# Reordering a gated-attention and expert kernel: decay issues, first loads, state scaling, transposes, and the last expert's second layer

## The chip, the cores and the metric

The kernel runs on one core of a Trainium2 chip. The metric is the device time of one execution in microseconds, from launch to end; lower is better. The core has TensorE (PE, with its weight loads shown apart as PEld), VectorE (DVE), ScalarE (ACT), GpSimd (POOL) and SyncE (SP, which here only issues DMAs). ACT and POOL issue DMAs too. Each engine takes its own instructions in order; semaphores hold an instruction until what it needs is there.

## The reference

Two blocks, one after the other, in float32. First a gated recurrence over 4 batches, 8 heads, 768 steps, head dimension 48:

```python
for t in range(S):
    state = alpha[:, :, t, :, None] * state + np.einsum('bhd,bhe->bhde', k[:, :, t], v[:, :, t])
    y[:, :, t] = np.einsum('bhd,bhde->bhe', q[:, :, t], state)
```

Its output, as 3072 rows of 384, goes through a layer of 8 experts with one expert for each row:

```python
expert_idx = np.argmax(x @ w_gate, axis=1)
gate_w = probs[np.arange(N), expert_idx]
# for each expert e, with its rows of x:
h = np.maximum(x_sorted[lo:hi] @ w1[e], 0.0)     # 384 -> 1024
y_sorted[lo:hi] = h @ w2[e]                      # 1024 -> 384
# back in the rows' own order, times gate_w
```

## The kernel before, in words

**The token loop.** The 768 steps of 4 batches are 24 tiles of 128 steps of one batch (8 heads side by side, 384 columns); tile s is chunk s // 4 of batch s % 4. The recurrence is done by chunks. For a tile, ACT takes the logarithm of alpha (`logs`, L387), PE sums it along the steps (`cums`, L393), ACT makes the running product `cp` and its inverse `icp` (L396, L397), and POOL multiplies q and k with them (`operands`, L434; the first tile on DVE). PE turns both (`transposes`, L444; ACT or DVE copies them out as kT and qT, L448 and L450), forms the scores (`scores`, L457), DVE masks them (L465), and PE adds to the PSUM tile `y` what comes from the earlier chunk's state (`read_state`, L484), from within the tile (`attend`, L494), and the keys times values for the new state (`keys_values`, L505). `result` (L513, ACT) copies y out as yT; `rows` (L531, PE) turns it into token rows `x` and gate logits in one PSUM bank; `gate`, `gate_weight` make the row's weight, and `keep_rows` (L556, ACT) copies x times that weight to `xs`, which SP stores to DRAM (L557).

The state's decay from one chunk to the next needs one row of `icp` and one of `cp` of every tile. `cums` sends them to a small tile `dec` with two DMAs issued by ACT (L405); POOL multiplies the rows (`decay_rows`, L413 and L414), PE turns them (L425), DVE copies the columns (`E`, L427), and `scale_state` (L472, POOL) scales the old state to U, which `read_state` uses.

The order is written out by hand. The loop runs over i from -4 to 23 with these stages of neighbouring tiles in each turn, and no scheduler moves them: in turn i, scores of tile i, transposes of i + 1, operands of i + 2, rows of i - 1, keep_rows of i - 2, running sums up to tile i + 5. Loads are issued by SP (`loads_for`), single tiles for the first two of each of alpha, k, q, v, then pairs of tiles (384 KB). `idle` (L589) is a filler: matmuls on zeros at the start. Between turns 4 and 14 SP also loads expert 0's weights, in parts, and DVE and POOL work out each row's place among the experts (`route`, `one_hots`).

**The experts.** After the loop come the experts in order of their row counts, with at most 424 rows for the first place and 8 fewer for each next (368 for the last). Expert 0's first 256 rows are done early. POOL gathers an expert's rows with indirect DMAs (L769); `turn` transposes them in blocks of 128 (L779, PE; copies L780 by DVE and ACT in turn, PSUM tag `tp` with two banks). Experts 1 to 7 do both layers with one level of a seven-product scheme for halves of the matrices: DVE makes sums of weights (`weight_sums`), of rows (`row_sums`) and of the hidden values (`th`), PE the products P1 to P7 (`chain`; L861 for layer 1, L917 for layer 2), ACT keeps some of them (u, p), DVE adds. Layer 2's third block of columns is done directly (L932). Its result is transposed (`zT`); `rows_out` turns it back to token rows (L962), ACT copies them (`zo`, L948), POOL scatters them to the output (L949). `rows_out` of an expert runs beside layer 1 of the next one; for the last it stands at the very end. After that a check skips a loop for overfull experts, which these data do not need.

Of the kernel before, what the change touches and what calls it, by code (L numbers as in the profile page):

```python
# [18 lines left out]
def kernel(  # L19
# [343 lines left out]
    with tc.tile_pool(name="ld", bufs=6) as ld, \  # L363
# [26 lines left out]
        def cums(s):  # L390
            c, b = cb(s)
            cum = ps.tile([C, 512], F32, name="cum")
            nc.tensor.matmul(cum[:, :Dm], lhsT=cum_m[:], rhs=st[s]["lna"][:], start=True, stop=True)  # L393
            cp = work.tile([C, Dm], F32, name="cp", bufs=6)
            icp = work.tile([C, Dm], F32, name="icp", bufs=6)
            nc.scalar.activation(icp[:], cum[:, :Dm], AF.Exp, scale=-1.0)  # L396
            nc.scalar.activation(cp[:], cum[:, :Dm], AF.Exp)  # L397
            st[s]["cp"], st[s]["icp"] = cp, icp


            for cc, i, row in ((c, 1, icp[0:1, :]), (c + 1, 0, cp[C - 1 :, :])):
                if 0 < cc < NB:
                    if cc not in decay:
                        decay[cc] = work.tile([B, 2, Dm], F32, name="dec", bufs=3)
                    nc.scalar.dma_start(decay[cc][b : b + 1, i, :], row)  # L405
# [33 lines left out]
        def transposes(s):  # L439
            d = st[s]  # L440
            for i, n in enumerate(("kT", "qT")):
                tp = ps.tile([C, NP, C], F32, name="tp", bufs=2)
                for p in range(NP):
                    nc.tensor.transpose(tp[:, p, :], pair(kqb[s % 3][:, i], p), ident[:])  # L444
                d[n] = work.tile([C, NP, C], F32, name=n)

                if s < B - 1 or i and s < NT - B - 2:
                    nc.vector.tensor_copy(d[n][:], tp[:])  # L448
                else:
                    nc.scalar.copy(d[n][:], tp[:])  # L450
# [116 lines left out]
        def sums_to(i):  # L567
            return {-2: 0, -1: 1, 0: 3, 1: 5}.get(i, -1 if i < 0 else min(i + 5, NT - 1))
# [6 lines left out]
        def loads(*wanted):  # L575
            for n, upto in wanted:
                while loaded[n] <= min(upto, NT - 1):
                    many = 1 if loaded[n] < 2 else 2
                    load(loaded[n], n, many)
                    loaded[n] += many  # L580

        def loads_for(i):
            loads(("a", sums_to(i + 1)), ("v", i), ("k", i + 2), ("q", i + 2))
# [7 lines left out]
        loads_for(-3)  # L591
        loads_for(-2)
# [8 lines left out]
        idle(4)  # L601
# [40 lines left out]
        def tiles(t0, n):  # L642
# [8 lines left out]
        on_gpsimd = {3 * B + 1: tiles(0, 3), 3 * B + 2: tiles(3, 3), 4 * B: tiles(6, 2), 5 * B: tiles(8, 3), 5 * B + 1: (13,)}  # L651
# [9 lines left out]
        for i in range(-4, NT):  # L661
            loads_for(i + 3)
# [43 lines left out]
            for s in sums[1:]:  # L706
                cums(s)
# [66 lines left out]
    def turn(g):  # L774
        g["xT"] = wk.tile([C, DB, CAP0], F32, name="xgT")
        for j, r in blocks(g):
# [3 lines left out]
            (nc.scalar.copy if j % 2 else nc.vector.tensor_copy)(g["xT"][:, :, j * C : j * C + r], tp[:, :, :r])  # L780

# [58 lines left out]
    def layer1(g, rows, ahead):  # L840
# [7 lines left out]
        def tile_parts(a):  # L848
# [19 lines left out]
            def res(i, k, at=None):  # L868
# [30 lines left out]
    def layer2(g):  # L899
# [28 lines left out]
        def rest(ahead, between):  # L928
# [9 lines left out]
            between()  # L938
            p5()
            p7()  # L940
# [17 lines left out]
    def rows_out(g):  # L958
        for j, r in blocks(g):
# [4 lines left out]
            yield  # L964

# [132 lines left out]
    turn(g0)  # L1098
# [9 lines left out]
    for i, g in enumerate(groups):  # L1108
        nxt = groups[i + 1] if i + 1 < E else None
        rest = []  # L1110

        def begin():
# [20 lines left out]
        def between():  # L1133
            if nxt:
                turn(nxt)
                row_sums(nxt)

        if i:
            rest[0](lambda: ahead(1, 2), between)
        else:  # L1140
            ahead(1)
            rest_layer2(g, 0)
            between()
            rest_layer2(g, 1)
            rest_layer2(g, 2)
        weights(i + 2, 2)
    for _ in rows_out(groups[-1]):
        pass
# [4 lines left out]
    with tc.If(nx > 0):  # L1153
        with tc.For_i(0, nx, 1) as i:
# [15 lines left out]
            turn(g)  # L1170
# [29 lines left out]
```

## Time and profile before

| | |
|---|---|
| median of the runs shown | 443.22 us (443.16 to 443.88) |
| profiled execution | 438.98 us |
| its span, first to last instruction | 436.9 us |
| mean granted TensorE clock | 0.991 |
| PE busy | 408.0 us, 93% of the span |
| DVE, ACT, POOL busy | 217.0, 172.5, 144.0 us |
| moved by DMA | 59.07 MB, of it 48.80 MB in 114,804 packets on the queue of SP |

The page divides the span into 40 slices and gives each engine's busy share in tenths, so a 9 is 90% or more; the row of the clock gives what TensorE was granted. The token loop fills about the first 155 us, the placing of the rows goes on to 171, the experts to 427, the last scatters and the program's end fill the rest. DMA is at nine tenths or more in slices 1 to 7 and at eight in the next three, which is the token loop up to about 109 us; PE is at nine tenths in nearly every slice after the first. A wait is put down to the instruction that ended it; waits on engines that are not the bound cost nothing by themselves.

### The profile page before, as it was taken

How to read it: one execution, taken by the hardware profiler on the slowest of the kernel's cores; microseconds unless marked ns; L12 is line 12 of the kernel's file. 1: busy time of each engine (PE TensorE's matmuls, PEld its weight loads, DVE VectorE, ACT ScalarE, POOL GpSimd, SP SyncE). 2: the span in 40 equal slices, each digit the busy share in tenths (PEclk: the TensorE clock that was granted, in tenths of full speed). 3: DMA queues.
4: the chain of work that ended last, by engine and by line, in shares of the span. 5: the costliest groups of instructions: out<-in, count | busy, mean ns of one | idle time of the engine just before them, and what ended most of it. 6: DMA issues, size and time to landing. Idle time of an engine off the chain costs nothing.

```text
span 436.9 us, 9317 instructions
## 1 busy us (share of the span) xinstructions
PE 408.0 (93%) x3566; PEld 347.5 (80%) x3566; DVE 217.0 (50%) x667; ACT 172.5 (39%) x457; POOL 144.0 (33%) x193
## 2 busy tenths in 40 slices
PE   8798998889999999999999999999999999999991
PEld 5576777767888786799879979969979979979870
DVE  5443544454456657364763472572573572573500
ACT  3464555545565441115314513513513513514411
POOL 2437454567739501712201420320330320201102
PEclk9999999999999999999999999999999999999996
DMA  9999999889573214754324155154154155000101
GB/s 176 200 206 189 204 228 216 210 196 216 135 138 84 74 56 145 281 184 169 104 96 165 46 194 163 40 198 157 43 199 161 39 196 162 35 2 18 33 0 52
DMA packets 119969, 59.07 MB, mean 135 GB/s; under 512 B 102806, under 2 KB 114159, under 8 KB 119924
## 3 DMA queue, kind: packets, MB, share of 16 engines
q1 hardware_dynamic: 114804, 48.80, 43.4%
q0 software_dynamic: 3424, 9.59, 6.3%
q8 instruction: 29, 0.48, 0.5%
q10 hardware_dynamic: 1696, 0.08, 0.2%
q14 instruction: 16, 0.13, 0.1%
HBM read 48.95 MB, written 9.58 MB: 134 GB/s over the span
## 4 chain that ended last, share of the span: by engine, by line
PE 71%; issue 7%; DMA 6%; ACT 4%; POOL 4%; DVE 3%; ACTq 2%; SPq 0%; POOLq 0%
PE pA L861 10%; PE pB L861 8%; PE pC L932 7%; PE pA L917 7%; PE pC L861 4%; PE sA L457 4%; PE x L531 4%; PE pB L917 4%; PE tp L444 4%; PE cum L393 3%; PE pC L917 2%; PE y L494 2%; ACTq L405 2%; DMA x_rows<-xs 2%; PE tp L779 2%
## 5 line engine op out<-in xcount | busy, mean ns | idle before, releaser
L949 POOL DMA_INDIRECT out_dram<-zo,sp x25 | 27.2, 1089 | 173.9 <-ACT zo L948 122.7
L805 ACT COPY u<-pA 128x208 f32<-128x208 f32 (+6 forms) x70 | 22.2, 317 | 65.8 <-PE pA L917 62.1
L184 DVE TENSOR_TENSOR h_sb<-pB,u 128x208 f32<-128x208 f32 (+6 forms) x56 | 20.2, 360 | 54.4 <-PE pB L861 41.5
L434 POOL TENSOR_TENSOR kqb<-k_sb,icp 128x384 f32<-128x384 f32 x23 | 23.0, 1001 | 52.3 <-PE y L505 18.9
L932 PE MATMUL pC<-h_sb,w 128*128 128x416 f32 (+6 forms) x112 | 38.0, 492 | 0.0
L932 PEld LDWEIGHTS pC<-h_sb,w 128*128 128x128 f32 x112 | 21.1, 190 | 13.6 <-issue 4.4
L538 DVE TENSOR_REDUCE lgn<-x 128x8 f32<-128x32 f32 x23 | 4.4, 192 | 51.3 <-PE x L531 45.6
L861 PE MATMUL pA<-t,s 128*128 128x208 f32 (+6 forms) x112 | 28.6, 337 | 0.6
L531 PE MATMUL x<-iw,yT 128*64 128x104 f32 x368 | 21.4, 258 | 7.8 <-ACT xs L556 7.7
L769 POOL DMA_INDIRECT xg<-x_rows,gp x25 | 25.9, 1035 | 7.6 <-issue 6.1
L457 PE MATMUL sA<-qT,kT 48*128 48x128 f32 x192 | 27.7, 285 | 0.1
L457 PE MATMUL sB<-qT,kT 48*128 48x128 f32 x192 | 27.7, 285 | 0.0
L861 PE MATMUL pA<-xgT,w 128*128 128x208 f32 (+6 forms) x112 | 27.7, 329 | 0.0
L444 PE MATMUL tp<-ident,kqb 128*128 128x128 f32 x192 | 26.4, 278 | 1.4 <-POOL kqb L434 1.4
L457 PEld LDWEIGHTS sA<-qT,kT 48*128 48x128 f32 x192 | 23.1, 187 | 3.5 <-DVE qT L448 0.7
L187 DVE TENSOR_TENSOR th<-h_sb,th 128x208 f32<-128x208 f32 (+6 forms) x56 | 20.2, 360 | 9.1 <-ACT h_sb L874 9.1
L531 PEld LDWEIGHTS x<-iw,yT 128*64 128x64 f32 x368 | 16.9, 136 | 9.8 <-ACT xs L556 9.4
L444 PEld LDWEIGHTS tp<-ident,kqb 128*128 128x128 f32 x192 | 20.7, 140 | 4.5 <-POOL kqb L434 2.1
L861 PE MATMUL pB<-t,w 128*128 128x208 f32 (+6 forms) x112 | 23.5, 332 | 0.2 <-DVE h_sb L184 0.2
L434 POOL TENSOR_TENSOR kqb<-q_sb,cp 128x384 f32<-128x384 f32 x23 | 23.0, 999 | 1.8 <-DMA q_sb<-in_q_dram 1.8
L861 PE MATMUL pC<-xgT,w 128*128 128x208 f32 (+6 forms) x112 | 23.1, 329 | 0.0
L457 PEld LDWEIGHTS sB<-qT,kT 48*128 48x128 f32 x192 | 23.1, 187 | 0.0
(237 smaller groups left out, 960.5 us busy)
## 6 DMA issues: line engine op xcount, KB each, us to landing
w<-in_moe_w_dram SPq DMA_DIRECT2D x14, 1536.0 KB, 7.3
x_rows<-xs SPq DMA_DIRECT2D x24, 192.0 KB, 2.9
a_sb<-in_alpha_dram SPq DMA_DIRECT2D x11, 384.0 KB, 4.9
k_sb<-in_k_dram SPq DMA_DIRECT2D x11, 384.0 KB, 5.4
q_sb<-in_q_dram SPq DMA_DIRECT2D x11, 384.0 KB, 6.0
v_sb<-in_v_dram SPq DMA_DIRECT2D x11, 384.0 KB, 4.4
w<-in_moe_w_dram SPq DMA_DIRECT2D x6, 256.0 KB, 3.5
w<-in_moe_w_dram SPq DMA_DIRECT2D x4, 384.0 KB, 3.5
```

The lines of the kernel that those rows point to most:

```text
L184: eng.tensor_tensor(out, a, b, op=ALU.add)
L187: eng.tensor_tensor(out, a, b, op=ALU.subtract)
L434: eng.tensor_tensor(by_half(kq[:, i]), d[n].rearrange("s (a p) d -> s a p d", a=2), d[e][:].rearrange("s (a p d) -> s a p d", a=2, p=NP), ...
L444: nc.tensor.transpose(tp[:, p, :], pair(kqb[s % 3][:, i], p), ident[:])
L457: nc.tensor.matmul(t[:, p, :], lhsT=d["kT"][r : r + D, p, :], rhs=d["qT"][r : r + D, p, :], start=True, stop=True,)
L531: nc.tensor.matmul(d["x"][o : o + HC, m, : D2 + E], lhsT=d["yT"][:, m // 2, m % 2, o : o + HC], rhs=iw[:, m, :], start=True, stop=True,)
L769: nc.gpsimd.indirect_dma_start(out=g["xg"][:r, j, :], out_offset=None, in_=x_d[:, :], in_offset=bass.IndirectOffsetOnAxis(ap=g["gi"](j, r) ...
L805: nc.scalar.copy(t[:, :m], bank["A"][:, :m])
L861: nc.tensor.matmul(out, lhsT=ops[n_][0], rhs=ops[n_][1], start=first and n_ == names[0], stop=True, skip_group_check=True,)
L917: nc.tensor.matmul(out, lhsT=lhs, rhs=rhs, start=first and f == 0, stop=True, skip_group_check=True)
L932: nc.tensor.matmul(d2[:, :n], lhsT=w2[:, f, 2 * C :], rhs=h[:, f, :n], start=(f == 0), stop=(f == FB - 1),)
L949: ins = nc.gpsimd.indirect_dma_start(out=out[:, :], out_offset=bass.IndirectOffsetOnAxis(ap=g["si"](j, r), axis=0), in_=zo[:r], in_offset= ...
```

## The change

- `cums` only makes the running products. The two decay DMAs of each tile are a function of their own (`decay_out`), called after `keep_rows` in the turn. Before the loop's turn 0 both sums of a turn are made one after the other, the second in the bank of x.
- The first loads are single tiles in an order written out by turn (8 tiles of alpha, 6 of k, 6 of q, 4 of v); from turn 2 on pairs as before. One filler fewer at the start, and the three of turn -1 are gone. Tile 0's kT is copied by ACT, not DVE.
- `scale_state` is called a turn ahead (except for the first tile of each chunk). Some one-hot products and one `rows_cols` change turn, one of them moves from turn 20 to turn 19 on DVE and one on POOL.
- `turn` stops after two blocks; the rest of it and the row sums come after the product P5 (for expert 0: after another third of its second layer).
- The last expert's layer 2 is done directly, by blocks of token rows: 3 blocks of 8 products with 384 columns, which ACT copies and POOL scatters as each is done. Six of the first block's products stand before the last two products of layer 1. The sums `th` and the weight sums for layer 2 of that expert are not made, nor its final transposes.
- Before the last expert's layer 1, GpSimd gets a `drain` instruction.

```diff
-        def cums(s):
-            c, b = cb(s)
-            cum = ps.tile([C, 512], F32, name="cum")
+        def cums(s, bank="cum"):
+            cum = ps.tile([C, 512], F32, name="cum", tag=bank)
...
             st[s]["cp"], st[s]["icp"] = cp, icp
+
+        def decay_out(s):
+            c, b = cb(s)
+            cp, icp = st[s]["cp"], st[s]["icp"]
...
-                if s < B - 1 or i and s < NT - B - 2:
+                if 0 < s < B - 1 or i and s < NT - B - 2:
                     nc.vector.tensor_copy(d[n][:], tp[:])
...
-            return {-2: 0, -1: 1, 0: 3, 1: 5}.get(i, -1 if i < 0 else min(i + 5, NT - 1))
+            return {-2: 1, -1: 1, 0: 3, 1: 5}.get(i, -1 if i < 0 else min(i + 5, NT - 1))
...
-        def loads(*wanted):
-            for n, upto in wanted:
-                while loaded[n] <= min(upto, NT - 1):
-                    many = 1 if loaded[n] < 2 else 2
-                    load(loaded[n], n, many)
-                    loaded[n] += many
+        singly = {-5: "aakq", -4: "kqav", -3: "akq", -2: "aav", -1: "kq", 0: "avakq", 1: "vkq"}
+
+        def load_next(n, many):
+            load(loaded[n], n, many)
+            loaded[n] += many
 
         def loads_for(i):
-            loads(("a", sums_to(i + 1)), ("v", i), ("k", i + 2), ("q", i + 2))
+            for n in singly.get(i, ""):
+                load_next(n, 1)
+            if i > 1:
+                for n, upto in ("a", sums_to(i + 4)), ("v", i + 3), ("k", i + 5), ("q", i + 5):
+                    while loaded[n] <= min(upto, NT - 1):
+                        load_next(n, 2)
...
-        loads_for(-3)
-        loads_for(-2)
+        loads_for(-5)
...
-        idle(4)
+        idle(3)
...
-            4 * B + 1: [(choose, 3), (ranks, 1)], 4 * B + 2: [(slots, 1, 4 * B)], 4 * B + 3: [(rows_cols, 1)],
-            5 * B: [(one_hots, nc.vector, 11, 12)], 5 * B + 1: [(one_hots, nc.vector, 14, 15)], NT - 2: [(choose, 4)],
+            4 * B + 1: [(choose, 3), (ranks, 1)], 4 * B + 2: [(slots, 1, 4 * B), (rows_cols, 1)],
+            4 * B + 3: [(one_hots, nc.vector, 11)],
+            5 * B: [(one_hots, nc.vector, 12, 14)], 5 * B + 1: [(one_hots, nc.vector, 15)], NT - 2: [(choose, 4)],
...
         for i in range(-4, NT):
-            loads_for(i + 3)
+            loads_for(i)
...
-            if -2 < i < 0:
-                idle(3)
             do(transposes, i + 1)
             sums = list(new_sums(i))
             for s in sums[:1]:
                 cums(s)
+            if i < 0:
+                for s in sums[1:]:
+                    cums(s, "x")
             do(gate_weight, i - 2)
             route(i)
             do(keep_rows, i - 2)
+            if i < 0 or len(sums) == 1:
+                for s in sums:
+                    decay_out(s)
...
             do(operands, i + 2)
-            if i < NT - 2:
+            if i % B == 0:
                 do(scale_state, i)
             if 0 < i + 1 < NT and (i + 1) % B == 0:
                 decay_rows((i + 1) // B)
+            elif i >= 0:
+                do(scale_state, i + 1)
...
-            if i == NT - 3:
-                for s in (NT - 2, NT - 1):
-                    scale_state(s)
...
-            for s in sums[1:]:
-                cums(s)
+            if i >= 0 and sums[1:]:
+                cums(sums[1])
+                for s in sums:
+                    decay_out(s)
             do(keys_values, i)
...
             (nc.scalar.copy if j % 2 else nc.vector.tensor_copy)(g["xT"][:, :, j * C : j * C + r], tp[:, :, :r])
+            if j == 1:
+                yield
...
                     nc.scalar.activation(h[:, FH + a, :n], h[:, FH + a, :n], AF.Relu)
+                    if last:
+                        return
...
-            between()
+            next(between, None)
             p5()
+            next(between, None)
             p7()
             c22()
             p34()
...
+    ready = [f for f in range(FB) if f % FH < FH - 1]
+
+    def rows_layer2(g, j, fs):
+
+        r = min(C, g["n"] - j * C)
+        if fs[0] == ready[0]:
+            t = "p" + "CAB"[j]
+            g["z"] = mps.tile([C, 512], F32, name=t, tag=t)
+        for f in fs:
+            nc.tensor.matmul(
+                g["z"][:r, :Dm], lhsT=g["h"][:, f, j * C : j * C + r], rhs=g["w2"][:, f, :],
+                start=(f == ready[0]), stop=(f == FB - 1), skip_group_check=True,
+            )
...
         def begin():
-            p1, tail = layer2(g)
-            p1()
-            rest.append(tail)
-
+            if last:
+                rows_layer2(g, 0, ready)
+            else:
+                p1, tail = layer2(g)
+                p1()
+                rest.append(tail)
+
+        if last:
+
+            nc.gpsimd.drain()
         if i:
-            layer1(g, beside(i), begin)
+            layer1(g, beside(i), begin, last)
...
-        def between():
+        def turned():
             if nxt:
-                turn(nxt)
+                yield from turn(nxt)
                 row_sums(nxt)
 
-        if i:
-            rest[0](lambda: ahead(1, 2), between)
+        between = turned()
+
+        if last:
+            for j, r in blocks(g):
+                rows_layer2(g, j, (*([] if j == 0 else ready), FH - 1, FB - 1))
+                scatter(g, j, r, g["z"][:r, :Dm])
+        elif i:
+            rest[0](lambda: ahead(*((1,) if i == E - 2 else (1, 2))), between)
         else:
             ahead(1)
             rest_layer2(g, 0)
-            between()
+            next(between)
             rest_layer2(g, 1)
+            next(between, None)
             rest_layer2(g, 2)
         weights(i + 2, 2)
-    for _ in rows_out(groups[-1]):
-        pass
```

More of the change, by code (lines that the diff above doesn't have):

```diff
@@ L647 @@
             2 * B + 3: [(slots, 0, 2 * B + 1)], 3 * B: [(rows_cols, 0)], 3 * B + 1: [(choose, 2)],
-            4 * B + 1: [(choose, 3), (ranks, 1)], 4 * B + 2: [(slots, 1, 4 * B)], 4 * B + 3: [(rows_cols, 1)],
-            5 * B: [(one_hots, nc.vector, 11, 12)], 5 * B + 1: [(one_hots, nc.vector, 14, 15)], NT - 2: [(choose, 4)],
+            4 * B + 1: [(choose, 3), (ranks, 1)], 4 * B + 2: [(slots, 1, 4 * B), (rows_cols, 1)],
+            4 * B + 3: [(one_hots, nc.vector, 11)],
+            5 * B: [(one_hots, nc.vector, 12, 14)], 5 * B + 1: [(one_hots, nc.vector, 15)], NT - 2: [(choose, 4)],
         }
-        on_gpsimd = {3 * B + 1: tiles(0, 3), 3 * B + 2: tiles(3, 3), 4 * B: tiles(6, 2), 5 * B: tiles(8, 3), 5 * B + 1: (13,)}
+        on_gpsimd = {3 * B + 1: tiles(0, 3), 3 * B + 2: tiles(3, 3), 4 * B: tiles(6, 2), 4 * B + 3: (8,), 5 * B: tiles(9, 2), 5 * B + 1: (13,)}
         counts_in = {2 * B + 2: 0, 4 * B + 1: 1}
@@ L838, in chain, with layer1 @@
         return p1, p2, p7, p6, p5, c22, p34
-    def layer1(g, rows, ahead):
+    def layer1(g, rows, ahead, last):
         n, m = g["n"], g["n"] // 2
@@ L1097 @@
     early_layer2(1, 0)
-    turn(g0)
+    for _ in turn(g0):
+        pass
     early_layer2(1, 1)
@@ L1110 @@
         rest = []
+        last = i == E - 1
         def begin():
-            p1, tail = layer2(g)
-            p1()
-            rest.append(tail)
+            if last:
[6 more added lines that the diff above has]
+            nc.gpsimd.drain()
         if i:
-            layer1(g, beside(i), begin)
+            layer1(g, beside(i), begin, last)
         else:
@@ L1169 @@
             gather(g)
-            turn(g)
+            for _ in turn(g):
+                pass
             plain(g)
```

## The prediction

> **What bounds the kernel now.** I read the table by stage first, then the waits of TensorE, then the timeline of one loop turn, then the end.
>
> Busy time of the engines in stretches of the span (us, then busy and count for PE, PEld, DVE, ACT, POOL; granted clock; DMA share; GB/s):
>
> ```profile
> 0.00:15.00 15.00, 12.69 (x70) 8.72 (x70) 8.14 (x18) 5.89 (x11) 3.47 (x11) 1.00 0.97 185
> ...
> 46.00:96.00 50.00, 44.47 (x718) 36.27 (x719) 23.45 (x83) 25.37 (x61) 24.02 (x30) 1.00 0.93 207
> 96.00:141.00 45.00, 43.96 (x710) 36.30 (x710) 24.39 (x86) 26.34 (x62) 31.56 (x46) 1.00 0.70 150
> ...
> 266.00:300.00 34.00, 33.58 (x188) 30.06 (x187) 17.59 (x47) 12.09 (x36) 7.83 (x7) 1.00 0.38 129
> ```
>
> PE is the bound nearly everywhere at clock 1.00. From 46 to 96 it idles 5.5 of 50 us while the transfers run at 0.93; an expert's turn (266 to 300) idles only 0.42. So time can come from the token loop, the start, and the end.
>
> TensorE's waits over the whole span (us, times, longest):
>
> ```profile
> PE x L531 <- ACT xs L556: 7.7, 11, 1.6
> PE tp L779 <- DVE xgT L780: 2.4, 7, 0.5
> PE y L484 <- POOL U L472: 1.9, 2, 1.0
> ```
>
> One loop turn, timeline:
>
> ```profile
> 58.83 0.48 ACT L397 ACTIVATE cp<-cum 128x384 f32<-128x384 f32 x1
> ...
> 58.97 0.51 ACTq L405 DMA_DIRECT2D dec<-icp  x1
> ...
> 59.56 0.55 ACTq L405 DMA_DIRECT2D dec<-cp  x1
> 59.77 0.53 PE L505 MATMUL y<-v_sb,kqb 128*48 128x48 f32 x16
> 60.21 0.58 ACT L556 ACTIVATE xs<-x,gw 128x384 f32<-128x384 f32 x1 [0.90 <-ACT cp L397]
> ...
> 60.85 0.40 PE L531 MATMUL x<-iw,yT 128*64 128x104 f32 x4 [0.55 <-ACT xs L556]
> ```
>
> PE is through with L505 at 60.30, but x is one PSUM bank, and ACT copies it out at 60.21 only because two decay issues stand ahead: PE idles 0.55. The end, timeline:
>
> ```profile
> 427.14 1.00 POOL L949 DMA_INDIRECT out_dram<-zo,sp  x1 [19.20 <-ACT zo L948]
> 428.45 0.98 POOL L949 DMA_INDIRECT out_dram<-zo,sp  x1 [0.31 <-issue]
> 429.74 0.96 POOL L949 DMA_INDIRECT out_dram<-zo,sp  x1 [0.30 <-issue]
> ```
>
> Three scatters, 1.30 us apart, all after the last matmul (427.46). The trace's own records go on, uncounted as busy: a POOL drain from 431.18 lasts 4.81 us, SyncE's waits are over at 433.0, the span ends at 436.9.
>
> **1. Rows copied ahead of the decay issues.** Nothing is added; two issues of 0.51 and 0.55 go behind L556. xs starts when cp ends, 59.25 instead of 60.21, and ends near 59.8, before PE's 60.30. What is queued behind the issues: L513 (yT), then the gate, the next logarithm, the copy of kT. L513 moves from 60.69 to about 60.9; its reader L531 is a whole turn later, and the kT copy has about 0.4 us of room. ACT's work in a turn is 3.75 + 1.06 = 4.8 us against PE's 5.55. The turns at 107.60 and 125.25 lack the wait and take 5.56 and 5.55; those with it take 6.16 to 6.20, those with a 1.30 us issue (92.37) up to 7.68. Turn by turn from tile 5 to 17, against 5.55 (5.99 with the decay transposes L425): 0.64+0.65+0.65+0.67+0.63+0.64+0.75+1.69+0.59+0.64+0+0+0.55 = 8.1 us.
> What is late next are the transfers. While expert 0's weights come (tiles 4 to 13), two turns ask for 8 loads, 2 row stores and 2 weight parts, 2.5 MB: 225 GB/s over 11.1 us. The stretch 46 to 96 moved 207 at share 0.93, the tens of us from 56 to 76 220 and 225. So the DMA has no reserve, but POOL's products run a turn ahead of their transposes, and a load of k issued at 51 is due only at about 67: some 10 us of cover. Between 0 given back and half the gain, I take 1.1: **-7.0**. The decay rows leave 0.6 us later and are needed 0.6 us sooner in each turn: from issue to L413 there were 3.9 us (52.77 to 56.63), now 2.7, against a landing of 2.6 to 4.0 in the loop. L413 may wait 1 us; POOL's slack there is 1.7 (its wait before L434 at 60.45). Nothing.
>
> **2. First loads singly, two decay sums at the start, fewer fillers.** Now v of tile 1 is the 11th issue and lands at 20.3 behind pairs not yet needed; PE waits 1.1 for it, POOL 3.2 and 1.8 for k and q. Singly, by need, at 192 KB per us: v1 at 16.4, k2 12.5, q2 13.5, the alpha of tiles 4 and 5 at 14.5 and 15.5. Following them through L387, L393, L434, tile 2's scores come at about 20.2 instead of 23.5 and tile 4's near 32.5 instead of 35.96. But up to q of tiles 6 and 7 the same 34 tile loads must land either way, near 36.5 to 37, and L472 for tile 4 stands behind that product on POOL: 38 instead of 39.6. So of some 3.5 us only 1.6 to 2 survive; the ends are 0 and -3.5.
> A rule against it: the Trainium skill (DMA: Bandwidth & Descriptors, Bandwidth) says to batch transfers to 1 MiB or more. Here 8 pairs of 384 KB become 16 singles. By the page's fixed 2.0 us for a DMA (Anatomy of one DMA, there for the gpsimd path) 8 more would be 16 us if nothing overlapped, and the change would lose. The row: the first 2 us stretches, mostly singles, move 192, 207 and 244 GB/s, the stretch 24 to 36, pairs only, 198. The page does not rule here: elements are 192 bytes in both, and loads overlap. Price: SP's issue, 0.8 to 1.5 us each, beside a saturated DMA.
> Four fillers (L589) go. The first eight records of them came every 0.47 us, the later six every 0.215: the clock doubled at about 5.5. The skill (TensorE: Matmul & The Clock Gate, the HAM clock gate) wants some 3.4 us of sustained work and takes the speed back after an idle window as long. PE's gaps become about 1 us near 6 and 8; the row 10 to 12, only 1.31 busy of 2, stayed at 1.00. By the row 0, by the rule +2 to +4. I take 0.5 of loss. Together **-1.5**.
>
> **3. States scaled a step ahead.** At tile 21 PE waits 1.0 for U; scaled one turn earlier it is there: **-1.0**. The other wait (0.9, tile 4) is in part 2. On POOL the product goes behind L434, which has cover. The moved one-hot products and slots stay within DVE's half-idle turns: 0.
>
> **4. Turns in two parts.** The third group of transposes at L779 waits 0.3 to 0.5 for DVE's copy (a bank of tp). With P5 (1.4 us) between, that wait goes, six experts and the first: 2.4. What is late next: the row sums, 5 x 0.37 on DVE, now stand ahead of c22, for which P4 waits. They end about 2.2 us after the second half of the turn; P7 and P3 give 2.8 us. Thin, but enough: **-2.3**; bounds 0 and -2.4, or +0.3 per expert if that cover fails.
>
> **5. Last place by token rows.** It drops seven groups of 8 half-products (L917, 1.41 each), L932 (5.11), transposes (2.15, gaps in it) and DVE's differences. It adds 24 products of 384 columns, two records each. The nearest row is L1052, the same shape: 8 records in 2.78 us, and L932's pitch 0.309 for 368 columns, so 0.3225 each, 15.5 us in all. From 409.12: block 0's ready six tiles to 413.0, P3 and P4 of layer 1 to 414.25, a gap of 0.4 for DVE's sum and ACT's relu, block 0 done 415.9, block 1 421.05, block 2 426.25. ACT copies (0.48), the last scatter starts at 426.95 instead of 429.74; the two others went out at 416.5 and 421.7. Then 1.4 us of POOL's end waits, now behind it instead of beside the earlier ones: the drain starts at 428.8 instead of 431.18. **-2.4**.
>
> **6. Early drain.** Put behind the last but one expert's scatters (375.65 is the last), it has POOL idle until 398.47: 21.7 us of cover for 4.8. Does it shorten the last one? Other POOL drains in the trace take 0.17 us after four memsets, and 0.11 and 0.05 after the long one; so the length is no constant. If it grows with the 58 indirect DMAs gone before, 6 are left: 0.5 us, and SyncE's end (last landing 1.75 us after the scatter, then 0.6) decides: -3.4. If it waits for the last scatter, nothing. It ended 3.5 us after that landing, which speaks for the first. I take **-2.5**.
>
> **Sum**: 7.0+1.5+1.0+2.3+2.4+2.5 = 16.7 us. The profiled execution took 438.98 (span 436.9), 4.2 under the median of the runs shown; the parts are differences, so profiled 422.3 and median **426.5**.
>
> **Rivals.** *The last drain stays long and half of part 2 is lost*: it may not depend on earlier DMAs (then part 6 does not do what it says): 443.2 - 13.4 = 430. *The transfers pace the loop*: no reserve at share 1.0 from 24 to 76. Loads and stores share one queue, so a late row store holds xs and PE waits at L531 again; half of part 1 goes, all of 2, half of 6: 443.2 - 10.5 = 433. Against it: the 10 us of cover. *Slower*: the same queue, worse. Singles use a two-tile buffer for one tile, so the loop enters its richest stretch with fewer tiles ahead; if the rate falls from 207 to under 170 GB/s until tile 14 (some 19 MB), those 100 us grow by more than 17, and all else is eaten: about 446. Nothing in the first slices shows such a rate. A granted clock below 0.95 would do the same (408 us of PE); it is 1.00 in every stretch of work.
>
> **Numbers.** Chances: 0.52 my sum (422 to 430), 0.23 the long drain, 0.14 the paced loop, 0.02 no change, 0.09 slower. A change within 0.2% (0.9 us) could not be told from none. Faster 0.89. The range, 421.5 to 435, takes in both faster rivals and part 2 and 6 at their better ends.
>
> **What would show it.** Loop turns of 5.55 and no wait of L531 for xs (1); tile 5's scores near 41.5 (2); no wait at L484 (3) nor L779 (4), and none new at P4; the last scatter 2.8 us nearer to the expert's P1 (5); a last drain under 1.5 us (6). I am wrong if L531 waits for xs behind a row store, if DMA waits of kqb appear after 46 us, or if PE waits at L917 for DVE.

## The result: 427.23 us, and the profile after

The changed kernel takes **427.23 us** (median of 4 executions, 423.88 to 430.02), beside 443.19 (442.69 to 443.88) before: a ratio of 0.9636, 95% interval 0.9564 to 0.9708. Its profiled execution took 427.84, the span 426.1, the mean granted clock 0.986. Two of all the executions, one of e3 (439.99 us) and one of the kernel before beside e0 (488.79), were in a slower state and are left out of the medians and ranges here. Line numbers shift: L531 is now L534, L556 is L559, L405 is L408, L484 is L487, L779 is L791, L949 is L966.

The same stretches as before (columns as there):

```profile
0.00:15.00 15.00, 12.24 (x94) 8.12 (x94) 7.54 (x17) 7.34 (x14) 5.41 (x13) 1.00 0.96 184
...
46.00:96.00 50.00, 50.00 (x818) 41.14 (x816) 28.05 (x93) 29.98 (x72) 30.86 (x42) 1.00 1.02 227
96.00:112.00 16.00, 13.81 (x164) 11.18 (x161) 5.66 (x17) 6.19 (x16) 9.41 (x14) 0.79 0.85 188
```

From 46 to 96 PE has no idle time left, where it idled 5.5 us. In the next 16 us it idles 2.2, and its clock is 0.79. What PE waits for, over the whole span:

```profile
PE x L534 <- ACT xs L559: 2.6, 2, 2.2
PE cum L392 <- ACT lna L387: 2.1, 2, 1.5
PE pB L1095 <- issue: 1.7, 1, 1.7
...
PE sA L460 <- ACT kT L453: 0.9, 1, 0.9
...
PE y L487 <- POOL U L475: 0.5, 1, 0.5
```

The eleven waits for xs have become one of 2.2 us and a short one; the seven waits of the transposes for DVE are gone; new are cum for lna (twice), L1095 (twice, 1.7 and 0.4 us) and the scores for kT. One loop turn:

```profile
54.74 0.49 ACT L395 ACTIVATE icp<-cum 128x384 f32<-128x384 f32 x1 [0.56 <-POOL er L416]
55.13 0.48 ACT L396 ACTIVATE cp<-cum 128x384 f32<-128x384 f32 x1
...
55.50 0.59 ACT L559 ACTIVATE xs<-x,gw 128x384 f32<-128x384 f32 x1
56.07 0.53 PE L508 MATMUL y<-v_sb,kqb 128*48 128x48 f32 x16
56.08 1.15 ACTq L408 DMA_DIRECT2D dec<-cp  x1
56.43 0.90 PE L534 MATMUL x<-iw,yT 128*64 128x104 f32 x16
```

xs now follows cp at once and is done at 56.09, before PE is through with L508, so L534 starts with no wait; a decay issue of 1.15 us stands behind it, and PE waits for nothing in this turn. Near 30 us it is otherwise. There two sums fall into one turn, and the decay issues of both tiles, four in a row, stand on ACT ahead of yT and the next logarithm (lna):

```profile
27.80 1.02 ACTq L408 DMA_DIRECT2D dec<-cp  x1
29.19 0.59 ACT L516 COPY yT<-y 128x512 f32<-128x512 f32 x1 [2.52 <-PE tp L447]
...
29.97 0.51 ACT L387 ACTIVATE lna<-a_sb 128x384 f32<-128x384 f32 x1
...
30.53 0.91 PE L392 MATMUL cum<-lna,cum_m 128*128 128x384 f32 x2 [1.49 <-ACT lna L387]
```

The four run from 25.91 to 28.82, the last for 1.02 us; yT starts 0.37 us behind it, and PE waits 1.49. In e0 and e1 the last one takes 1.50 and 1.54 us, yT starts 0.37 and 0.38 behind it, and PE waits 1.97 and 2.01. In e3 the issues go out two and two, and PE has no such wait; e4, with the same loads as e3 and four in a row, has it (1.30). What the profile names as the end of yT's idle time differs from run to run (L447 here, a DMA of dec in e0 and e1), so this cause is read from the order and the times; no run undoes it alone. The end:

```profile
411.66 1.01 POOL L966 DMA_INDIRECT out_dram<-zo,sp  x1 [9.24 <-ACT zo L965]
416.82 0.99 POOL L966 DMA_INDIRECT out_dram<-zo,sp  x1 [4.15 <-ACT zo L965]
422.02 0.95 POOL L966 DMA_INDIRECT out_dram<-zo,sp  x1 [4.22 <-ACT zo L965]
```

The scatters go out as their blocks are done, and the span ends 4.1 us after the last one starts, where it was 7.15.

Where the loop lost time again is at 100 us. SyncE's issues, ACT's copy and PE's product there, in order of time:

```profile
89.59 0.58 ACT L559 ACTIVATE xs<-x,gw 128x384 f32<-128x384 f32 x1
90.18 2.98 SPq L379 DMA_DIRECT2D v_sb<-in_v_dram  x1
...
93.26 3.17 SPq L379 DMA_DIRECT2D k_sb<-in_k_dram  x1
...
96.53 1.34 SPq L379 DMA_DIRECT2D q_sb<-in_q_dram  x1
...
97.96 1.59 SPq L560 DMA_DIRECT2D x_rows<-xs  x1
...
103.14 0.58 ACT L559 ACTIVATE xs<-x,gw 128x384 f32<-128x384 f32 x1 [2.54 <-DMA x_rows<-xs]
...
103.77 1.52 PE L534 MATMUL x<-iw,yT 128*64 128x104 f32 x16 [2.19 <-ACT xs L559]
```

Rows written at 89.59 to 90.17 go to memory only by an issue at 97.96, because three loads stand ahead of it on SyncE's queue, and their issues take 7.5 us. xs has two buffers, so ACT waits for that store and PE for ACT. Then the clock falls:

```profile
104.00:106.00 2.00, 2.00 (x22) 1.75 (x20) 0.63 (x3) 0.59 (x3) 0.00 (x0) 0.50 1.05 211
106.00:108.00 2.00, 2.00 (x18) 1.77 (x15) 0.00 (x0) 0.56 (x3) 0.00 (x0) 0.50 1.30 248
```

It stays at 0.50 for 6.83 us. Two turns (scores of tile 15 to those of tile 17) take 16.94 us; without a wait they take 11.33. The difference of 5.6 us is the wait of 2.19 and half of 6.83.

### The profile page after: what moved, and what is told of

Its sections match the earlier page's. It is cut to its first block, busy times and chain, and to the rows that moved or that the text cites. A ratio compares the mean times of both kernels' runs of the same rounds, so it can differ in the third digit from the quotient of the medians.

```text
span 426.1 us, 9224 instructions
## 1 busy us (share of the span) xinstructions
PE 408.6 (96%) x3525; PEld 344.9 (81%) x3525; DVE 208.0 (49%) x643; ACT 171.4 (40%) x453; POOL 144.1 (34%) x193
## 4 chain that ended last, share of the span: by engine, by line
PE 80%; DMA 7%; issue 6%; ACT 2%; DVE 1%; POOL 1%; SPq 1%; ACTq 0%; POOLq 0%
PE pA L875 10%; PE pB L875 8%; PE pC L948 7%; PE pA L933 7%; PE sA L460 5%; PE y L497 5%; PE tp L447 4%; PE pB L933 4%; PE pC L875 4%; PE x L534 4%; PE cum L392 3%; PE y L487 2%; DMA x_rows<-xs 2%; PE pC L933 2%; PE tp L791 2%
## 5 line engine op out<-in xcount | busy, mean ns | idle before, releaser
L966 POOL DMA_INDIRECT out_dram<-zo,sp x25 | 27.0, 1081 | 169.6 <-ACT zo L965 118.9
L948 PE MATMUL pC<-h_sb,w 128*128 128x416 f32 (+5 forms) x96 | 32.9, 496 | 0.0
L460 PE MATMUL sA<-qT,kT 48*128 48x128 f32 x192 | 28.6, 291 | 0.9 <-ACT kT L453 0.9
L460 PE MATMUL sB<-qT,kT 48*128 48x128 f32 x192 | 28.6, 291 | 0.0
L948 PEld LDWEIGHTS pC<-h_sb,w 128*128 128x128 f32 x96 | 18.1, 190 | 12.0 <-issue 4.4
L447 PE MATMUL tp<-ident,kqb 128*128 128x128 f32 x192 | 26.9, 284 | 0.3 <-DVE kqb L437 0.3
L447 PEld LDWEIGHTS tp<-ident,kqb 128*128 128x128 f32 x192 | 21.6, 144 | 3.2 <-issue 0.9
L534 PE MATMUL x<-iw,yT 128*64 128x104 f32 x368 | 21.5, 260 | 2.8 <-ACT xs L559 2.6
L392 PE MATMUL cum<-lna,cum_m 128*128 128x384 f32 x48 | 21.1, 521 | 2.2 <-ACT lna L387 2.1
L888 ACT ACTIVATE h_sb<-h_sb 128x416 f32<-128x416 f32 (+6 forms) x28 | 14.8, 530 | 20.5 <-DVE h_sb L184 20.1
```

Source lines behind the costliest of these rows:

```text
L460: nc.tensor.matmul(t[:, p, :], lhsT=d["kT"][r : r + D, p, :], rhs=d["qT"][r : r + D, p, :], start=True, stop=True,)
L534: nc.tensor.matmul(d["x"][o : o + HC, m, : D2 + E], lhsT=d["yT"][:, m // 2, m % 2, o : o + HC], rhs=iw[:, m, :], start=True, stop=True,)
L948: nc.tensor.matmul(d2[:, :n], lhsT=w2[:, f, 2 * C :], rhs=h[:, f, :n], start=(f == 0), stop=(f == FB - 1),)
L966: ins = nc.gpsimd.indirect_dma_start(out=out[:, :], out_offset=bass.IndirectOffsetOnAxis(ap=g["si"](j, r), axis=0), in_=zo[:r], in_offset= ...
```

## The experiments

All times are medians; "before" is the kernel before on the same chip in the same session, and each ratio is to it.

| kernel | us (lowest to highest) | before | ratio, 95% interval |
|---|---|---|---|
| e0, changed kernel again | 425.96 (424.75 to 426.59) | 443.32 | 0.9604, 0.9569 to 0.9638 |
| e1, three buffers for xs | 422.41 (420.40 to 426.22) | 443.32 | 0.9549, 0.9499 to 0.9599 |
| e7, stores ahead of loads | 423.84 (422.31 to 425.16) | 443.32 | 0.9554, 0.9517 to 0.9592 |
| e2, no early drain | 429.92 (428.90 to 431.33) | 443.32 | 0.9707, 0.9668 to 0.9745 |
| e3, rows first, alone | 435.40 (433.31 to 435.43) | 444.37 | 0.9779, 0.9747 to 0.9812 |
| e4, first loads as before | 428.36 (426.52 to 431.30) | 444.37 | 0.9637, 0.9599 to 0.9675 |
| e5, last place as before | 427.78 (426.86 to 429.21) | 444.37 | 0.9628, 0.9597 to 0.9659 |
| e6, turn in one part | 431.56 (429.30 to 433.84) | 444.37 | 0.9709, 0.9674 to 0.9744 |
| e9, one gather later | 423.01 (422.12 to 424.21) | 443.89 | 0.9532, 0.9512 to 0.9553 |
| e10, scaling as before | 424.96 (421.94 to 427.50) | 443.89 | 0.9582, 0.9550 to 0.9615 |

Two more, e8 and the kernel before itself, ran once each: 425.87 and 445.39 us.

A second table cuts the profiled executions at marks that all kernels share: tile 5's scores, those of tiles 15, 17 and 23, the end of expert 0's first layer, expert 6's last scatter, and the span's end. "First layer" is its last part, 48 products of one line (L1064, in the changed kernel L1095), from the end of the first to the end of the last.

| us | before | before again | changed | e0 | e1 | e3 |
|---|---|---|---|---|---|---|
| tile 5's scores start | 43.12 | 43.03 | 40.26 | 40.52 | 41.81 | 41.90 |
| tiles 5 to 15 | 64.48 | 65.95 | 56.53 | 57.12 | 55.88 | 55.87 |
| tiles 15 to 17 | 11.55 | 11.55 | 16.94 | 15.50 | 11.33 | 12.01 |
| tiles 17 to 23 | 32.01 | 32.02 | 30.73 | 30.72 | 30.66 | 31.79 |
| first layer of expert 0 | 6.70 | 11.10 | 10.14 | 9.39 | 8.47 | 11.32 |
| from there to expert 6's scatter | 219.25 | 220.18 | 217.31 | 216.87 | 216.88 | 221.08 |
| from there to the span's end | 30.08 | 30.08 | 24.72 | 24.85 | 24.78 | 30.07 |

### e0, e1, e7: is it the row store that costs the loop its gain?

> The changed kernel once more, as the yardstick for the kernels beside it. If the wait for the rows' buffers near 101 us and the half clock after it are a property of this schedule, the stretch from tile 15's scores to tile 17's takes about 17 us again (8.4 + 8.5) where two other turns take 10.9, and the median is near 427. If they were an accident of the one profiled execution, the stretch takes 11 to 13 us, and executions without it lie near 422.

e0: the stretch took 15.50 us, with this wait for xs and 3.41 us of half clock:

```profile
104.84 1.51 PE L534 MATMUL x<-iw,yT 128*64 128x104 f32 x16 [2.42 <-ACT xs L559]
```

It is the schedule, then: each of the seven profiled kernels with the changed loop, two buffers for xs and loads ahead of the store has a wait of 1.3 to 2.5 us for xs, though at different tiles (at 104 to 106 in five, at 82 in e6, at 59 in e5).

```diff
-            xs = work.tile([C, NP, D2], F32, name="xs")
+            xs = work.tile([C, NP, D2], F32, name="xs", bufs=3)
```

> The changed kernel with three buffers for the gated rows xs in place of two, so that ACT can write the next rows while the store of rows two tiles back still waits in SyncE's queue. Theory A (the late row store holds xs, TensorE stands still at L534, and the clock falls to half after it): the wait of x for xs is gone, tiles 15 to 17 take 5.5 to 6 us each with the clock at 1.00, some 5 us less: 422 to 423 us. Rival B (the transfers' rate paces this stretch, the row store is only where it shows): the wait moves to the loads of k, q or v, and the time stays within 1 us of the changed kernel, 426 to 428. Rival C (the clock falls by itself): no wait, but a half clock near 100 us remains, 424 to 427.

The same place with three buffers:

```profile
92.41 4.16 SPq L379 DMA_DIRECT2D v_sb<-in_v_dram  x1
...
96.67 1.33 SPq L379 DMA_DIRECT2D k_sb<-in_k_dram  x1
...
98.09 1.45 SPq L379 DMA_DIRECT2D q_sb<-in_q_dram  x1
99.64 3.14 SPq L560 DMA_DIRECT2D x_rows<-xs  x1
101.38 0.59 ACT L559 ACTIVATE xs<-x,gw 128x384 f32<-128x384 f32 x1
...
102.31 0.90 PE L534 MATMUL x<-iw,yT 128*64 128x104 f32 x16
```

The store leaves as late as in the changed kernel (99.64, for rows made at 90.48 to 91.07, behind issues of 4.16, 1.33 and 1.45), but ACT and PE no longer wait for it. The table by stretches, for the same 16 us:

```profile
96.00:112.00 16.00, 16.00 (x264) 13.24 (x262) 7.92 (x26) 9.67 (x25) 12.68 (x18) 1.00 1.01 208
```

PE full, clock 1.00, and the DMA moves more than in the changed kernel's same stretch (208 against 188 GB/s). So the rate of the transfers (rival B) did not pace the loop; a buffer held by the order of a queue did, and theory A holds. The profile is 4.9 us shorter than e0's and the median 3.55 lower, though the two ratios' intervals overlap; e9 (below), which has three buffers too and issues its gathers when e1 does, has an interval clear of e0's. Rival C (the clock by itself) falls: e1, e9 and e10 have three buffers and no such wait, and all three keep the clock at 1.00 from 96 to 112.

```diff
-            loads_for(i)
+            if i < 2:
+                loads_for(i)
...
             do(keep_rows, i - 2)
+            if i >= 2:
+                loads_for(i)
```

> The changed kernel with the loads of each turn from the third on issued after the row store instead of before it, so that on SyncE's queue a row store stands ahead of the turn's loads. Theory A: the store of a tile is no longer held behind loads that take 1.3 to 3.2 us each to issue, xs comes free in time, and the wait at L534 near 101 us goes: 422 to 424 us. Rival B: each load now leaves later, by the time that SyncE waits for xs, so the loads of k and q come late and TensorE waits for kqb instead: 427 to 431.

The wait for xs is gone here too: 11.33 us for the two turns. But tile 5's scores came at 43.64, 3.1 us later than in e0: y waits 1.82 us for U in the start, after POOL had waited 2.01 for a load of k, and 3.41 us of half clock follow. So both theories named a part: the buffer is freed, and loads that leave later cost the start. The third buffer does the first without the second.

### e2, e8: what the early drain saves

```diff
-        if last:
-            nc.gpsimd.drain()
```

> The changed kernel without the early drain of GpSimd. Theory (a drain's length grows with the indirect DMAs issued since the last one): the last drain takes 4.5 to 5 us instead of 1.2, and the span ends 3 to 3.6 us later after the last scatter, about 430.5 us. Rival (a drain waits only for the last scatter to land, and the short one came from the shorter last place): the last drain stays under 2 us and the time within 0.5 us of the changed kernel.

From expert 6's last scatter to the end it takes 29.07 us without the early drain, 24.85 with it in e0 and 24.72 in the changed kernel: 4.2 to 4.4 us, and 4.0 by the medians. GpSimd's records at the end of the span, start and length:

```
                 INC_SWDGE_SEM    DRAIN
before           429.79  1.359    431.18  4.809
e2, no drain     420.03  1.358    421.42  4.809
changed          423.42  0.318    423.77  1.205
```

Two instructions get shorter by it: the drain by 3.6 us, and the one ahead of it by 1.04, which I had not known of. The early drain itself is no shorter than the late one was: it takes 5.70 us from 370.27 on, in a stretch where GpSimd, after a scatter at 370.50, starts nothing until 393.05. The rival falls, since e2 has the new last place and a long drain.

```diff
+            if i == 20:
+                nc.gpsimd.drain()
...
-        if last:
+        if i in (1, 2, 4, 6, 7):
             nc.gpsimd.drain()
```

> The changed kernel with other drains of GpSimd: one in turn 20 of the token loop, ahead of any indirect DMA, and one each before experts 1, 2, 4, 6 and 7. If a drain's length grows with the indirect DMAs issued since the last one (58 in 4.8 us, 6 in 1.2 us: some 0.4 us and 0.07 us for each), the one in the loop takes under 0.5 us, and the others take 1 to 2.5 us by the number before them. If it is a fixed price of 5 us after any indirect DMA, each of them takes 4.5 to 5.7 us.

Neither: they took 2.15 us in the loop, and 6.31, 6.18, 9.15, 9.05 and 3.03 before the experts, with 11, 6, 15, 14 and 5 indirect DMAs since the drain before; the last one took 1.48 with 7. Length does not go by that number, and the one with none before it was not short. These records lie over gathers that start after them, so they may hold waits of other kinds. Shown is only that a drain before the last expert makes the last one short; what its length counts stays open.

### e3: the rows copied first, alone

The kernel before, with its two decay issues moved behind `keep_rows` and nothing else.

```diff
             do(keep_rows, i - 2)
+            for s in sums[:1]:
+                decay_out(s)
...
             for s in sums[1:]:
                 cums(s)
+                decay_out(s)
```

> The kernel before with one thing of the change: the copy of the gated rows stands ahead of the two decay issues on ACT. The sum gave this part 8.1 us, less 1.1 given back to the transfers. If it stands on its own, the waits of L531 for xs (7.7 us in 11 places) fall under 1 us, the turns take 5.5 to 5.6, and the time is 7 to 8 us under the kernel before. If the transfers or the two buffers of xs take it back here too, a wait of over 2 us for xs comes up near tile 16 or earlier, and the gain is 2 to 5 us.

The ratio is 0.9779, some 9.8 us (8.4 to 11.2 by the interval; 9.0 by the medians), more than the 7 to 8 expected. From tile 5 to 17 it takes 67.88 us against 76.03, 8.2 less, and tile 5's scores come 1.2 sooner. The turns from tile 5 to 15 take 55.87 us, 5.59 each; L534 waits for xs 0.5 us once. This one edit is more than half of all that the change brings. Why e3, with the same two buffers and the same order of loads and stores there, escapes the wait of 2 us was not settled. In its profile the same store leaves at 98.30, again behind three loads, and lands 4.0 us later; in the changed kernel it took 5.1, in e0 5.2.

### e4, e5, e6, e10: the other parts undone

```diff
-        singly = {-5: "aakq", -4: "kqav", -3: "akq", -2: "aav", -1: "kq", 0: "avakq", 1: "vkq"}
+            loads(("a", sums_to(i + 1)), ("v", i), ("k", i + 2), ("q", i + 2))
...
-            loads_for(i)
+            loads_for(i + 3)
```

> The changed kernel with the first loads in the order and in the pairs of the kernel before; the two decay sums at the start and the fewer fillers stay as changed. The trace of the changed kernel has tile 5's scores 2.9 us earlier than before. If the single loads made that, tile 5's scores come near 43 again. Behind them two ends are open: the 2.9 us carry through to the end (428 to 430 against 426), or the loop meets its wait near 101 us whatever the start was, that wait shrinks by what the start lost, and the time is within 1 us of the changed kernel.

Tile 5's scores came at 42.51, 2.0 us later than in e0. At tile 15 0.7 us was left of it, and the two turns after that took 15.50 as in e0. The medians stand 16.0 us under before against e0's 17.4, so 1.3 us, and the two intervals overlap. Nor is the start clear: the nine profiled kernels with the changed start (e7 apart) have tile 5's scores anywhere from 40.26 to 42.16, and e4 has 3.41 us of half clock from 11.63 on, worth up to 1.7. The single loads bring between 0.3 and 2.3 us at the start, with the clock in it, and no gain at the end that is clear of noise.

```diff
-        last = i == E - 1
+        last = False
...
-        if last:
+        if i == E - 1:
             nc.gpsimd.drain()
...
+    for _ in rows_out(groups[-1]):
+        pass
```

> The changed kernel with the last expert's second layer as in the kernel before (halves, then transposes, three scatters together); the early drain stays. The sum gave this part 2.4 us: 428 to 429. In the traces the last scatter starts 18.3 us after the last expert's first matmul in the changed kernel against 20.6 before, but in the changed kernel 1.4 us of GpSimd's end work stand behind it that stood between the scatters before: so 1 us is the lower end, 427.

From expert 6's last scatter to the end: 27.12 us. With the numbers before (30.08), without the drain (29.07) and with both (24.8), the two parts separate: the new last place alone brings 1.0, the early drain alone 3.0, both 5.3. They add more than their sum: in e2 the last scatter starts 2.3 us nearer to expert 6's scatter than before, but the drain starts 2.78 us behind it instead of 1.44, because the 1.36 us instruction and the end's register work stand one behind the other there.

```diff
-            if j == 1:
+            if False:
                 yield
```

(and the second call of the generator made harmless.)

> The changed kernel with the transposes of a turn in one part again. The sum gave this part 2.3 us (seven waits of L791 for DVE's copy of xgT of 0.3 to 0.5 us). If that is right, those waits return with 2.0 to 2.4 us in all, and the time is 428 to 428.5 against 426. If the order of the sums on DVE gave it back elsewhere, the time is within 0.5 us of the changed kernel.

```profile
PE x L534 <- ACT xs L559: 2.7, 2, 2.1
PE pB L1095 <- DVE h_sb L1100: 2.5, 1, 2.5
PE cum L392 <- ACT lna L387: 2.4, 2, 1.8
PE tp L791 <- DVE xgT L792: 2.3, 7, 0.4
```

The waits are back, 2.3 us in seven. The time rose by 4.5 rather than 2.3 (12.8 under before against e0's 17.4). In its profile the stretch after expert 0's first layer is 4.4 us longer than in e0; half clock from 183.8 to 187.8 explains 1.9 of that, and 2.4 are left for the waits. The rest stands in the loop and in expert 0, where waits and half clock fell otherwise than in e0.

```diff
-            if i % B == 0:
+            if i < NT - 2:
                 do(scale_state, i)
...
-            elif i >= 0:
-                do(scale_state, i + 1)
...
+            if i == NT - 3:
+                for s in (NT - 2, NT - 1):
+                    scale_state(s)
```

(on e1)

> The changed kernel with three buffers for xs, and with the states scaled in the turn that reads them, as before. The sum gave this part 1.0 us: a wait of about 1.0 us of y for U at tile 21 returns, and the time is 423 to 424 against 422.4. The rival is that the wait at tile 4, which the product of k and q sets, is all that is seen: no more than 0.3 us of difference.

The wait at tile 21 does not return. Before and in e3 that turn takes 6.15 and 6.14 us, in the changed kernel 5.08, in e10 5.25. Tiles 17 to 23 take 30.94 against 30.66 in e1. So scaling a turn ahead brings 0.3 us, and the other 0.8 come from something that e10 keeps; the one-hot product that left POOL's turn 20 is the nearest candidate: before and in e3 three of them stand on POOL ahead of the next U, in e10 two, and one takes 1.1 us, as much as the wait was. It was not tried alone. The medians (424.96 and 422.41) cannot tell this much.

### The kernel before again, and e9: a stop that the first profile did not have

> The kernel before once more, for a second profile of it. The profiled execution of it took 438.98 us, the others 442 to 447. All kernels with a faster loop show a stop of TensorE of 1 to 3 us among the last products of the first layer of expert 0 (L1095 in the changed kernel, L1064 in this one), with the clock at one half for 3.4 or 6.8 us after it in five of them; the profile of before has none. If the stop belongs to this place of the program, other executions of before have it too, and this one takes 442 to 446 with 3 us or more lost there. If the faster loop makes it, this profile has none, and its longer time is spread elsewhere.

It took 445.39, and it has the stop:

```profile
190.65 0.33 DVE L1069 TENSOR_SCALAR h_sb<-pB 128x168 f32<-128x168 f32 x1 [5.61 <-remote]
190.72 0.51 ACT L1072 ACTIVATE h_sb<-pC 128x168 f32<-128x168 f32 x2 [4.03 <-remote]
191.03 2.01 PE L1064 MATMUL pB<-xgT,w 128*128 128x168 f32 x6 [3.17 <-DVE h_sb L1069]
```

DVE and ACT both stand still for 4 to 6 us in the midst of copies out of PSUM that PE's records show long finished, and PE then waits for them; the products of L1064 took 11.10 us, in the first profile 6.70. So the stop belongs to this place of the program and not to the faster loop, and the first profile, 438.98 us, was of an execution that escaped it. The stop explains 4.4 of the 6.4 us between the two; half clock, from 95.54 and from 191.11 on for 3.41 us each, is most of the rest.

```diff
-        if i + 2 < E:
+        if 0 < i and i + 2 < E:
             gather(groups[i + 2])
...
             rest_layer2(g, 0)
+            gather(groups[2])
```

(on e1)

> The changed kernel with three buffers for xs, and with the gather of the third group's token rows (four indirect DMAs on GpSimd) moved from beside the last products of expert 0's first layer to behind a third of its second layer. In every trace with a stop of TensorE at L1095, the stop begins as these four gathers are issued and ends about 1 us after the last of them. If they make it, it goes, or moves with them into L1111: without it the time is 420 to 421 against 422.4. If it is tied to the place in the program (an instruction fetch of 16 KB stands there in each trace) it stays at L1095, and the time is as it was.

Nothing was learned of the gathers: nothing else stands in POOL's queue there, so it issued them from 171.46 to 175.23, as in e1 (171.25 to 175.03). The stop was there (3.1 us). Its cause stays open.

## Why the prediction held, and where its terms were off

**The median, 426.5 against 427.23 and 425.96.** The runs show parts 1, 4, 5 and 6 at work, part 2 within wide limits and part 3 to a third. That the total came out so near was luck, because the misses nearly cancel: the loop kept 3.0 us less than part 1's 7.0, while the start (1.3 more than summed), expert 0's first layer (1.0, in no part), the experts (0.6), the end (0.5) and tile 21 (0.3) brought more. Against the second profile of before (span 443.3), the changed kernel's (426.1) is shorter by 2.8 to tile 5, 4.0 from there to tile 17, 1.3 to tile 23, 1.0 in expert 0's first layer, 2.9 to expert 6's last scatter and 5.4 behind it; 0.1 is lost in between.

**The basis.** I took the 4.2 us between the profiled execution of before and its median as a constant to add, and put the profiled changed kernel at 422.3; it took 427.84. The stop of up to 4.6 us is what the first profile lacked and the 13 others have. So the 4.2 were right for the median and wrong for the profile, and that they were right was luck too: I had not looked for their cause.

**1, rows first: 8.1, less 1.1 to the transfers.** The gain was of the right size: from tile 5 to 17 e3, which has this part alone, takes 67.88 us against 76.03, that is 8.2; e1 takes 67.20. The term that was mis-sized is the 1.1 given back: against e1 it was 6.3 us in the profiled execution (73.47), 5.4 in e0, and 1.5 to 4.7 in the five other kernels with this wait. I had named the place (a row store behind loads on SyncE holds xs) as a rival and set it aside for "10 us of cover". That cover is the loads' own, until k is needed. The store has another, set by the two buffers of xs: the rows made by 90.17 had to be in memory at 100.60, when ACT wanted their buffer again, and that is 10.4 us. Of these the queue took 7.8 before the issue, and the landing 5.1 after it. I also priced a wait by its own length, where about half its price was the clock behind it (3.4 of 5.6 us in the changed kernel, 1.7 of 4.2 in e0). What the decay issues hold up in their new place I had followed in a plain turn only; where two sums fall into one turn, near 30 us, PE waits 1.5 us of cum for lna.

**2, first loads: 1.5.** Tile 5's scores came at 40.3 and 40.5, 1 us better than the 41.5 named. But e3, with the loads and fillers of before, has them at 41.90, so 1.2 of it is part 1's, and 1.4 to 1.6 are left, which is the size that was named. At the end e4 gives 1.3, not clear of noise. The 0.5 for the fillers was not seen in the changed kernel, where the clock was 1.00 from 5.0 us on; e4, with fewer fillers and the old loads, has half clock at 11.63. What came next is that wait near 30 us, 1.3 to 2.3 us long in all eleven kernels with the new decay issues; in e5 and e9 half clock came after it.

**3, scaling ahead: 1.0.** The wait went, 6.15 to 5.08 us in that turn, but e10 puts only 0.3 us down to this edit. The step that failed is the moved one-hot products, taken at 0: the other 0.8 come from something that e10 keeps, most likely the one that left POOL's turn 20.

**4, turns in two parts: 2.3.** e6 brings the waits back to the tenth, and from expert 0 to expert 6 e0 and e1 are 2.4 us shorter than the first profile of before, all three without half clock there.

**5 and 6, last place 2.4, drain 2.5.** Together 5.4 against 4.9. Singly the last place was over-sized (1.0: its gain of 2.3 at the last scatter is eaten by 1.34 more until the drain) and the drain under-sized (4.2 to 4.4 on top of it), because one further instruction of GpSimd's end gets shorter. One reading of the end was a little off: the first of the three scatters before starts at 427.14, just ahead of the last matmul's end at 427.46. Nothing in the sum hangs on it.

**The rivals.** The long drain fell with e2. The paced loop came true in its mechanism at a price of 1.5 to 6.3 us, and not in its reason: e1 moves as much per us and does not wait. In the changed kernel, e0 and e1 no load of k, q or v held PE in the loop after 46 us.

## What to carry over

When an edit takes a wait out of a loop, ask of each buffer in it which queue frees it and what stands ahead of that store; cover that loads have says nothing about stores on the same queue. Ask the same of an issue that is moved: what stands behind it in its new place. Price a PE wait of 2 us with what the clock may take after it (1.7 or 3.4 us here). And take a second profile of a kernel whose profiled execution lies 1% from its median, before summing against it.

**Faster than both kernels** was e1, the changed kernel with one more buffer: 422.41 us, ratio 0.9549 (0.9499 to 0.9599). That it beats the changed kernel rests on e9 too (0.9512 to 0.9553 against e0's 0.9569 to 0.9638).

## What was not expected of the hardware

- **The clock.** Half clock came behind waits of PE of 1.62 us (before again, 94.16), 2.19 (changed), 2.29 (e9), and not behind 2.52 (e2) or 3.13 (e8). Within the work it always lasted 3.41 or 6.83 us, and in each of the 14 profiles all changes of the clock lie whole multiples of 3.41 us apart (in the changed kernel at 103.95, 110.78, 182.46 and 185.87). Cut the spans at that pitch up to the last matmul, and the puzzle goes: of 1,675 pieces at full clock, PE was by its records idle for 46% or more in 20, and 17 of these were followed by half clock; of the other 1,655 none was. The wait in e2 fell into two pieces (34 and 40% idle), and so did e8's (56 and 35%, one of the three exceptions). The Trainium skill (TensorE: Matmul & The Clock Gate, The HAM clock gate) says that the clock falls after at least one idle window of about 3.4 us; its length agrees with the stretches seen, its condition does not, as pieces that were half idle were enough. By the rule the changed kernel's wait at 103.77 would have cost 2.2 us; it cost 5.6.
- **GpSimd's end** takes 6.2 us (1.36 and 4.81) after the 58 indirect DMAs without an earlier drain, alike to a nanosecond in before and e2, and 1.5 to 3.0 us (e5) where a drain ran some 50 us earlier.
- **The stop in expert 0's first layer**, up to 4.6 us longer than the 6.70 us without it, in 13 of 14 profiled executions, begins within 1 us of a 16 KB instruction fetch in twelve of them. But such a fetch stands there without a stop in the first profile of before too, and in e10 it came 4.8 us after the stop had begun, so it is not shown to be the cause.
